# Weight sums made and split ahead, gated sums on VectorE, eight x tiles: a talking-heads attention with a two-layer feed-forward

## The chip, the core and the metric

The kernel runs on one core of one Trainium2 chip. The metric is the device time of one execution in microseconds; where several runs were timed, their median. The profile is of one execution, and its span runs from the first to the last instruction.

## What is computed

Four batches, 12 heads, 448 positions, head size 64; then 1792 tokens of width 768 and a hidden width of 2048, all in float32:

```python
scores = scale * np.matmul(q, k.transpose(0, 1, 3, 2))
scores = np.einsum('bhij,hg->bgij', scores, w_pre)
scores = scores - np.max(scores, axis=-1, keepdims=True)
attn = np.exp(scores)
attn = attn / (np.sum(attn, axis=-1, keepdims=True) + 1e-09)
attn = np.einsum('bhij,hg->bgij', attn, w_post)
x = np.matmul(attn, v)            # heads side by side: [1792, 768]
...
h = x @ w_in
g = np.where(h >= 1, h, np.where(h <= -1, 0.0, (h + 1) ** 2 / 4))
return g @ w_out
```

The two weights of the feed-forward, w_in and w_out, arrive as float64.

## The kernel before, in words

The order of the work on every engine is the order in which the code issues it: nothing is rescheduled. Each engine runs its own instructions strictly in that order, and nearly all transfers are issued by SyncE (SP in the profile), whose queue is in order too: a transfer that waits for a tile to come free holds all that are issued after it. A tile's name stands for a ring of buffers; whoever takes a new one waits until the one before it in that buffer has been read.

**Attention** runs over 16 tiles of up to 120 query positions, cut into 48 groups of mostly four blocks. A block's scores come back from the buffer `ssb` through `load_s` (a ring of eight), are mixed over heads (`pre`), get a maximum and exponentials, and are mixed again (`post`); `pv` makes x, which goes to DRAM as `xd`. Beside this, w_in and part of w_out are converted from float64 to float32 (`conv_units`, then `late_units` during the first product), and written to the DRAM arrays `wid` and `wod`.

**Split products.** TensorE multiplies float32 values as a high and a low part. A split is one ScalarE operation (high part) and one VectorE operation (low part, the value less its high part); a product is then three matmuls: low by high, high by low, high by high.

**The first product**, x @ w_in, runs in two passes (`ph`) over the halves of the tokens. A pass has 16 steps, one for each 128 of the hidden columns; a step is two halves of 448 tokens (`ffn1`), 18 matmuls each, and the gate (`gate`: one ScalarE, two VectorE operations per half), whose output goes to the tiles `gq`. Step s also splits the weights of step s+2 (`split_w`: wh on ScalarE, wl on VectorE) and loads those of step s+3 (`load_w`, tile wi). The x tiles of a pass are six for each half; `load_x` brings a raw tile xr from `xd`, through a ring of two, and `split_x` makes xh and xl. Those of pass 1 are loaded and split in step 15, when pass 0's are no longer read. Products go to eight PSUM banks in turn.

**The second product**, g @ w_out, is done as seven products of quarter matrices (`PROD`: A are quarters of the gated values, B of w_out). Each product runs through 14 items: two halves of the inner dimension, seven pairs of token blocks each. An item is 12 matmuls of 384 columns (`mults`). `prep_s` prepares an item's left side three items ahead: the split into sgh and sgl, and, for some products, a sum or difference of quarters on GpSimd (POOL), of which two overwrite a quarter of `gq` that later products read. `prep_t` prepares the right side in four quarters z per product: it loads one to four pieces of `wod`, adds them up on VectorE and splits the sum with `split_pair`, at items 1 and 4 of each half, four quarters ahead. `evict` adds a finished product into the results and stores them.

## Time and profile before

| | us |
|---|---|
| median of 3 timed runs | 989.46 (987.29 to 989.78) |
| profiled execution | 985.9 |
| its span, first to last instruction | 984.2 |
| attention, until the first product runs alone | 0 to 471.5 |
| first product, pass 0 | to about 583 |
| first product, pass 1 | to 716.1 |
| second product | 719.7 to 980.4 |
| mean granted TensorE clock (1.00 is 2.4 GHz, 0.50 is 1.2 GHz) | 0.967 |

Times in the profile count from the span's start. A matmul's shown duration is its way through the array, and matmuls overlap; their pace is read from the distance of their starts. A window counts each instruction that lies in it even partly.

### The profile page before, as it was taken

The numbers are of one execution on the slowest core, as the hardware profiler recorded it, in microseconds if no ns is written. First come the engines' busy times: TensorE is split into PE (matmuls) and PEld (weight loads), VectorE is DVE, ScalarE is ACT, GpSimd is POOL, SyncE is SP. The second block draws the span as 40 slices with busy tenths as digits, with TensorE's granted clock in tenths as the row PEclk, the third lists the DMA queues.
The fourth block names the chain that finished last, engine by engine and source line by source line (L and its number), as shares of the span: only waits on it lengthen the run. The fifth ranks groups of instructions, "written<-read, shape, count | busy, mean of one in ns | idle before, by whom it ended". The sixth has DMA issues, their size and how long they took to land.

```text
span 984.2 us, 17942 instructions
## 1 busy us (share of the span) xinstructions
PE 927.3 (94%) x6554; PEld 817.5 (83%) x6554; DVE 644.3 (65%) x1128; ACT 505.3 (51%) x1112; POOL 278.9 (28%) x309
## 2 busy tenths in 40 slices
PE   8999999999999999998999988999989877999758
PEld 7788888788887888887999976999989777998658
DVE  4878786776878777754576744444399567656344
ACT  4777777677776777665454423223245123434021
POOL 0343343433443333321122210000069686000000
PEclk9999999999999999999999996999999978999979
DMA  8758567865787657525666533121121342312442
GB/s 170 226 165 222 178 198 224 214 203 180 220 235 208 188 186 229 173 79 157 185 188 201 168 106 105 49 65 49 33 65 33 129 149 91 106 57 97 145 153 72
DMA packets 139930, 145.09 MB, mean 147 GB/s; under 512 B 63300, under 2 KB 131652, under 8 KB 139844
## 3 DMA queue, kind: packets, MB, share of 16 engines
q1 hardware_dynamic: 137060, 143.27, 48.5%
q10 hardware_dynamic: 2784, 0.69, 0.4%
q8 instruction: 52, 0.85, 0.4%
q14 instruction: 34, 0.28, 0.1%
HBM read 81.80 MB, written 23.59 MB: 107 GB/s over the span
## 4 chain that ended last, share of the span: by engine, by line
PE 79%; DMA 10%; DVE 5%; ACT 2%; issue 2%; SPq 1%; POOL 1%; DVEq 0%; ACTq 0%
PE ps_h L409 23%; PE ps_a L232 14%; PE ps_o L520 13%; PE ps_l L201 8%; PE ps_x L248 8%; PE ps_s L156 6%; DMA wo<-wod 5%; PE ps_l L199 5%; DVE wo L484 2%; DMA xr<-xd 1%; DMA s<-ssb 1%; DVE sgl L499 1%; ACT wh L376 1%; DVE wl L377 1%; PE ps_t L139 1%
## 5 line engine op out<-in xcount | busy, mean ns | idle before, releaser
L222 POOL TENSOR_SCALAR wr<-wpost,rs 120x120 f32<-120x120 f32 x180 | 113.3, 646 | 297.8 <-DVE rs L218 274.6
L520 PE MATMUL ps_o<-wh,sgl 128*128 128x384 f32 x392 | 139.5, 356 | 36.7 <-DVE sgl L499 25.6
L232 PEld LDWEIGHTS ps_a<-wr,e 120*112 120x112 f32 x1440 | 154.6, 177 | 6.9 <-issue 5.0
L232 PE MATMUL ps_a<-wr,e 120*112 120x120 f32 (+1 forms) x1440 | 155.4, 266 | 0.0
L409 PE MATMUL ps_h<-xh,wl 128*128 128x448 f32 x384 | 143.3, 373 | 5.6 <-ACT xh L395 5.6
L409 PE MATMUL ps_h<-xl,wh 128*128 128x448 f32 x384 | 143.3, 373 | 0.4 <-DVE xl L396 0.4
L409 PE MATMUL ps_h<-xh,wh 128*128 128x448 f32 x384 | 142.6, 371 | 0.0
L520 PE MATMUL ps_o<-wl,sgh 128*128 128x384 f32 x392 | 138.5, 353 | 2.4 <-DVE wl L377 2.4
L211 ACT ACTIVATE e<-ps_l,nm 120x448 f32<-120x448 f32 x180 | 112.8, 632 | 52.6 <-DVE nm L205 52.4
L520 PE MATMUL ps_o<-wh,sgh 128*128 128x384 f32 x392 | 137.6, 351 | 0.0
L520 PEld LDWEIGHTS ps_o<-wh,sgl 128*128 128x128 f32 x392 | 79.1, 202 | 40.9 <-DVE sgl L499 28.6
L205 DVE TENSOR_REDUCE nm<-ps_l 120x1 f32<-120x448 f32 x180 | 102.9, 616 | 9.3 <-PE ps_l L201 7.7
L417 ACT ACTIVATE a<-ps_h,c 128x448 f32<-128x448 f32 x64 | 40.1, 633 | 120.4 <-PE ps_h L409 73.6
L418 DVE TENSOR_TENSOR mx<-ps_h,a 128x448 f32<-128x448 f32 x64 | 39.9, 623 | 91.6 <-ACT a L417 91.0
L201 PE MATMUL ps_l<-s,wpre 120*120 120x448 f32 x196 | 95.4, 570 | 4.6 <-DMA s<-ssb 3.3
L302 POOL TENSOR_TENSOR wt<-wt,wk 128x384 int32<-128x384 int32 x64 | 70.8, 1109 | 92.3 <-DVE wt L298 54.3
L234 ACT ACTIVATE aT<-ps_a 112x480 f32<-112x480 f32 x180 | 95.6, 594 | 2.2 <-PE ps_a L232 1.8
L376 ACT ACTIVATE wh<-wo 128x768 fp32r<-128x768 f32 x28 | 23.6, 842 | 121.5 <-DVE wo L484 93.1
L409 PEld LDWEIGHTS ps_h<-xh,wl 128*128 128x128 f32 x384 | 73.6, 192 | 14.3 <-ACT xh L395 8.2
L248 PE MATMUL ps_x<-aT,v 112*64 112x120 f32 (+1 forms) x1536 | 83.8, 262 | 0.2 <-ACT aT L234 0.2
L520 PEld LDWEIGHTS ps_o<-wl,sgh 128*128 128x128 f32 x392 | 78.7, 201 | 3.9 <-DVE wl L377 3.9
L499 DVE TENSOR_TENSOR sgl<-gq,sgh 128x512 fp32r<-128x512 f32 x84 | 77.3, 953 | 4.5 <-ACT sgh L498 4.4
(83 smaller groups left out, 1576.5 us busy)
## 6 DMA issues: line engine op xcount, KB each, us to landing
s<-ssb SPq DMA_DIRECT2D x172, 210.0 KB
wo<-wod SPq DMA_DIRECT2D x56, 384.0 KB
wraw<-in_moe_w_in_dram SPq DMA_DIRECT2D x32, 384.0 KB
wi<-wid SPq DMA_DIRECT2D x32, 384.0 KB
raw<-in_moe_w_out_dram SPq DMA_DIRECT2D x20, 384.0 KB
wid<-wt SPq DMA_DIRECT2D x32, 192.0 KB
wod<-wt SPq DMA_DIRECT2D x32, 192.0 KB
v<-in_v_dram SPq DMA_DIRECT2D x12, 448.0 KB
```

The costliest lines, as they stand in the source:

```text
L156: nc.tensor.matmul(out=ps[s][:n], lhsT=qt[t][x][r, hp, :n], rhs=kt[b, hp][y][r, :], start=(m == 0), stop=(m == 2))
L201: nc.tensor.matmul(out=lps[m], lhsT=wpre[:k], rhs=x[:k], start=True, stop=True)
L205: nc.vector.tensor_reduce(out=nm, in_=lps[m], axis=AX.X, op=ALU.max, negate=True)
L211: nc.scalar.activation(out=e, in_=ps, func=AF.Exp, bias=nm, accum_out=sm[:, j:j + 1])
L222: nc.gpsimd.tensor_scalar_mul(out=w[:, :, :ni], in0=wpost[:, :, :ni], scalar1=rs[:, j:j + 1])
L232: nc.tensor.matmul(out=ps[:, r, :ni * H], lhsT=e[:, r * KP:(r + 1) * KP], rhs=w[:, :, :ni], start=True, stop=True)
L234: nc.scalar.activation(out=aT[t][:, :, :, c:c + ni], in_=ps[:, :, :ni * H].rearrange("q r (h i) -> q r h i", h=H), func=AF.Copy)
L248: nc.tensor.matmul(out=ps[s * D:(s + 1) * D, m, :n], lhsT=vt[b, g][:, 2 * m + s, r * D:(r + 1) * D], rhs=a[:, r, 4 * g + 2 * m + s, :n], s ...
L302: nc.gpsimd.tensor_tensor(out=st["t"], in0=st["t"], in1=st.pop("k"), op=ALU.add)
L409: nc.tensor.matmul(out=ps[:, :NH], lhsT=w[:, k], rhs=x, start=(c == 0), stop=(c == last))
L499: nc.vector.tensor_tensor(out=lo, in0=src, in1=hi.bitcast(F32), op=ALU.subtract)
L520: nc.tensor.matmul(out=o, lhsT=x[:, f, :], rhs=y[:, c], start=first and f == 0 and m == 0, stop=hf == 1 and f == 3 and m == 2, skip_group_ ...
```

## The change

1. *Weight sums.* In pass 1 of the first product, from step 17 to step 29, `t_units` makes the sums of quarters of w_out that four of the seven products need: eight rows of four units. A unit adds two raw tiles in place, so that each sum grows out of the one before, splits it into a tile x (ring of two), and the unit after it stores both parts to a new DRAM array `td`; the raw tile that it used up is loaded for the next row. In the second product `prep_t` only loads the two parts for these products. For the three products with a single quarter the load is issued two quarters earlier (`load_t`), and the split stays.
2. *Sums of gated values* are made on VectorE, one for each item of five of the seven products, three of them after and two before the split; which quarter is overwritten by what is rearranged so that each product needs one sum.
3. *x tiles.* For pass 1 eight raw x tiles are loaded at the end of step 12 (six in a new ring, two in the old), the last four during step 15 into the new ring. For pass 0 the first half's x tiles are loaded behind the score loads of a group, and the second half's all together into a ring of six, and split later. The conversion of w_out now ends at step 12.
4. *The join.* The first items and quarters of the second product are prepared in steps 30 and 31 ahead of the gates of those steps, and the lead is four items instead of three. The split tiles of gated values have seven buffers instead of six.

```diff
+    td = dram.tile([7, 2, NF // 4, 128, 2, CW], F32, name="td")
...
     def prep_t(k, z):
-        f = 2 * z
-        terms = PROD[k][2]
-        t = traw(terms[0][0], f, "r", 2)
-        for name, sg in terms[1:]:
-            y = traw(name, f, "ra", 2)
-            nc.vector.tensor_tensor(out=t, in0=t, in1=y, op=ALU.add if sg > 0 else ALU.subtract)
-        tset[k, z] = split_pair(t)
+        if len(PROD[k][2]) == 1:
+            tset[k, z] = split_pair(tset[k, z])
+            return
+        tset[k, z] = [pool['w'].tile([128, DM], F32R, tag="w" + c, name="w" + c, bufs=4) for c in "hl"]
+        for c, t in enumerate(tset[k, z]):
+            nc.sync.dma_start(out=t.bitcast(F32), in_=td[k, c, z].rearrange("p f d -> p (f d)"))
...
+        def store():
+            if made:
+                k, f, x = made.pop()
+                nc.sync.dma_start(out=td[k, :, f // 2, :, f % 2, :].rearrange("h p d -> p h d"), in_=x.bitcast(F32))
+
+        def make(f, k, o, u, v, sg, nxt):
+            def unit():
+                if k == 3 and f == 0:
+                    for name in ("B12", "B22", "B11", "B21"):
+                        load(name, f)
+                x = pool['tq'].tile([128, 2, CW], F32R, tag="x", name="x", bufs=2)
+                o_ = raws[o]
+                nc.vector.tensor_tensor(out=o_, in0=raws[u], in1=raws[v], op=ALU.add if sg > 0 else ALU.subtract)
+                nc.scalar.activation(out=x[:, 0], in_=o_, func=AF.Copy, scale=2.0 ** -8)
+                nc.vector.scalar_tensor_tensor(out=x[:, 1], in0=o_, scalar=2.0 ** -8, in1=x[:, 0].bitcast(F32),
+                                               op0=ALU.mult, op1=ALU.subtract)
+                store()
+                made.append((k, f, x))
+                for name in nxt:
+                    load(name, f + 1)
+            return unit
+
+        for f in range(NF // 2):
+            us.append(make(f, 3, "B12", "B22", "B12", -1, ()))
+            us.append(make(f, 2, "B11", "B12", "B11", 1, ("B12",)))
+            us.append(make(f, 4, "B22", "B22", "B11", -1, ("B22",)))
+            us.append(make(f, 6, "B21", "B11", "B21", -1, ("B11", "B21")))
+        us.append(store)
...
+        def sums(o, x, y, op):
+            nc.vector.tensor_tensor(out=o, in0=x, in1=y, op=op)
         if kind == "S2":
             src = pool['f2'].tile([128, 4, 128], F32, tag="s2", name="s2", bufs=2)
-            nc.gpsimd.tensor_tensor(out=src, in0=a22, in1=a11, op=ALU.subtract)
+            sums(src, a22, a11, ALU.subtract)
+        if kind == "S1":
+            sums(a21, a21, a22, ALU.add)
...
         if kind == "A11":
-            nc.gpsimd.tensor_tensor(out=a11, in0=a11, in1=a21, op=ALU.subtract)
+            sums(a11, a11, a21, ALU.subtract)
         if kind == "A12":
-            nc.gpsimd.tensor_tensor(out=a21, in0=a21, in1=a22, op=ALU.add)
-        if kind == "S2":
-            nc.gpsimd.tensor_tensor(out=a12, in0=a12, in1=src, op=ALU.subtract)
+            sums(a12, a12, a22, ALU.subtract)
+        if kind == "S3":
+            sums(a12, a12, a11, ALU.add)
...
-            cvs(ncv * (s + 0.5) / (NF - 1))
-            gate(s, 0, h)
+            cvs(ncv * (s + 0.5) / NV)
+            if s == te:
...
+                load_t(*tops[0])
+                load_t(*tops[1])
             if last:
                 for kk in range(KDM):
                     split_x(ph + 1, 0, kk)
-                    z = kk + 2
-                    load_x(ph + 1, z // KDM, z % KDM)
-            if s == NS - 1:
-                prep_t(0, 0)
-            gate(s, 1, h1)
+                    if kk >= 2:
+                        load_x(ph + 1, 1, kk, "xq", KDM)
+            if s >= te:
+                prep_t(*tops[s - te])
+                load_t(*tops[s - te + 2])
+                for j in ((0, 1), (2,))[s - te]:
+                    prep_s(j)
+            gate(s, 0, h)
+            if s >= ts:
+                tuns(ntu * (s - ts + 0.5) / (te - ts))
...
+            gate(s, 1, h1)
+            if s >= ts:
+                tuns(ntu * (s - ts + 1) / (te - ts))
+            cvs(ncv * (s + 1) / NV)
+            if f == NV - 1 and ph + 1 < PH:
...
+                for kk in range(KDM):
+                    load_x(ph + 1, 0, kk, "xq", KDM)
+                for kk in range(2):
+                    load_x(ph + 1, 1, kk)
```

Here NV is 13, ts 17 and te 30.

How instructions move is seen in the order on the engines. On SyncE's queue at the end of attention (s10 are score tiles, xr raw x tiles, wi a weight tile of the first product), before:

```order
L387 DMA xr_6395<-xd_75 128x448
L387 DMA xr_6397<-xd_75 128x448
L370 DMA wi_6399<-wid_76 128x768
L180 DMA s10_6401<-ssb_5936 108x1x448
L180 DMA s10_6403<-ssb_5936 120x1x448
L180 DMA s10_6405<-ssb_5936 108x1x448
L264 DMA xd_75<-xo_6158 768x1x120
```

and after the change:

```order
L374 DMA wi_6395<-wid_76 128x768
L184 DMA s10_6397<-ssb_5936 108x1x448
L184 DMA s10_6399<-ssb_5936 120x1x448
L184 DMA s10_6401<-ssb_5936 108x1x448
L391 DMA xr_6403<-xd_75 128x448
L391 DMA xr_6405<-xd_75 128x448
L268 DMA xd_75<-xo_6158 768x1x120
```

The two x loads have moved from ahead of the last three score loads to behind them.

On VectorE a step of pass 1 of the first product (wl is the low part of a weight tile, mx and gq the gate), before:

```order
L377 SCALAR_TENSOR_TENSOR wl_7962<-wi_7911,wh_7961 128x768
L418 TENSOR_TENSOR mx_7968<-ps_h_7923,a_7967 128x448
L419 SCALAR_TENSOR_TENSOR gq_6745<-a_7967,mx_7968 128x448
L418 TENSOR_TENSOR mx_7973<-ps_h_7942,a_7972 128x448
L419 SCALAR_TENSOR_TENSOR gq_6745<-a_7972,mx_7973 128x448
```

and after, with b the raw quarters and x the split sums:

```order
L381 SCALAR_TENSOR_TENSOR wl_7974<-wi_7923,wh_7973 128x768
L422 TENSOR_TENSOR mx_7980<-ps_h_7935,a_7979 128x448
L423 SCALAR_TENSOR_TENSOR gq_6749<-a_7979,mx_7980 128x448
L517 TENSOR_TENSOR b_7984<-b_7986,b_7984 128x384
L519 SCALAR_TENSOR_TENSOR x_7992<-b_7984,x_7992 128x384
L517 TENSOR_TENSOR b_7988<-b_7984,b_7988 128x384
L519 SCALAR_TENSOR_TENSOR x_7996<-b_7988,x_7996 128x384
L422 TENSOR_TENSOR mx_8004<-ps_h_7954,a_8003 128x448
L423 SCALAR_TENSOR_TENSOR gq_6749<-a_8003,mx_8004 128x448
L517 TENSOR_TENSOR b_7986<-b_7986,b_7988 128x384
L519 SCALAR_TENSOR_TENSOR x_8008<-b_7986,x_8008 128x384
```

Two or three units now stand between the gates of a step, each an addition and, behind ScalarE's high part, a low part.

On VectorE at the join of the two products (wl from wo is the low part of a weight quarter, sgl that of an item), before:

```order
L418 TENSOR_TENSOR mx_8710<-ps_h_8671,a_8709 128x448
L419 SCALAR_TENSOR_TENSOR gq_6748<-a_8709,mx_8710 128x448
L377 SCALAR_TENSOR_TENSOR wl_8717<-wo_8714,wh_8716 128x768
L418 TENSOR_TENSOR mx_8721<-ps_h_8690,a_8720 128x448
L419 SCALAR_TENSOR_TENSOR gq_6748<-a_8720,mx_8721 128x448
L377 SCALAR_TENSOR_TENSOR wl_8734<-wo_8731,wh_8733 128x768
L499 TENSOR_TENSOR sgl_8738<-gq_6741,sgh_8737 128x512
L499 TENSOR_TENSOR sgl_8743<-gq_6741,sgh_8742 128x512
```

and after, from step 31 on:

```order
L381 SCALAR_TENSOR_TENSOR wl_8970<-wo_8903,wh_8969 128x768
L555 TENSOR_TENSOR sgl_8976<-gq_6745,sgh_8975 128x512
L545 TENSOR_TENSOR gq_6745<-gq_6745 128x4x128
L422 TENSOR_TENSOR mx_8981<-ps_h_8931,a_8980 128x448
L423 SCALAR_TENSOR_TENSOR gq_6752<-a_8980,mx_8981 128x448
L422 TENSOR_TENSOR mx_8986<-ps_h_8950,a_8985 128x448
L423 SCALAR_TENSOR_TENSOR gq_6752<-a_8985,mx_8986 128x448
L555 TENSOR_TENSOR sgl_8996<-gq_6745,sgh_8995 128x512
L545 TENSOR_TENSOR gq_6745<-gq_6745,gq_6749 128x4x128
```

The second quarter and the third item stand ahead of the last two gates; the fourth item (sgl_8996) stands behind them.

## Rows read from the trace of the kernel before

**Rows 1.** The page, busy time of each engine and its share of the span

```profile
PE 927.3 (94%) x6554; PEld 817.5 (83%) x6554; DVE 644.3 (65%) x1128; ACT 505.3 (51%) x1112; POOL 278.9 (28%) x309
```

**Rows 2.** Windows, first product: PE and weight load busy (count), clock, DMA share, GB/s

```profile
471.50:582.75 111.25, 111.25 (x549) 103.11 (x550) 1.00 0.57 175
471.50:716.11 244.61, 238.63 (x1134) 216.68 (x1134) 0.97 0.37 113
```

**Rows 3.** Timeline of PE, end of the first product: start, duration

```profile
715.74 0.37 PE L409 MATMUL ps_h<-xh,wh 128*128 128x448 f32 x1
```

**Rows 4.** Chain of waits at the pass change: start, duration, what

```profile
587.64 2.54 DMA xr<-xd
...
590.21 0.58 ACT xh L395
...
590.81 0.64 DVE xl L396
```

**Rows 5.** Windows, second product, a stretch without waits; columns as rows 2

```profile
843.00:873.00 30.00, 30.00 (x175) 30.00 (x175) 1.00 0.28 90
```

**Rows 6.** Chain of waits from the last gate to the end

```profile
716.20 0.64 ACT a L417
...
789.75 1.67 POOL s L495
...
793.93 4.96 DMA wo<-wod
...
802.36 1.75 DVE sgl L499
...
888.15 1.87 DMA out_dram<-osb
...
918.29 0.97 DVE wo L484
...
919.28 3.09 DMA wo<-wod
...
923.50 0.85 ACT wh L376
...
925.34 0.60 DVE sgl L499
925.94 0.47 DVE u L552
...
980.44 0.55 DVE u L555
```

**Rows 7.** Waits of PE from 400 us: total, times, longest

```profile
PE ps_l L201 <- DMA s<-ssb: 2.6, 1, 2.6
```

**Rows 8.** Waits of SyncE's queue, 420 to 475 us; columns as rows 7

```profile
SPq L387 <- DVE xl L396: 22.3, 5, 10.1
```

**Rows 9.** Windows, end of attention: PE, PEld, DVE, ACT, POOL busy, clock, DMA share, GB/s

```profile
445.88:451.19 5.31, 2.73 (x42) 2.42 (x41) 0.97 (x3) 4.27 (x11) 0.00 (x0) 1.00 0.85 252
451.19:455.19 4.00, 4.00 (x9) 2.33 (x10) 3.41 (x8) 1.01 (x3) 2.84 (x3) 0.57 0.68 169
```

**Rows 10.** Chain of waits, the round of attention before that

```profile
442.05 0.94 PE ps_l L201 x2
...
444.36 1.51 PE ps_a L232 x15
```

**Rows 11.** Windows inside pass 0 and pass 1; columns as rows 9

```profile
500.00:560.00 60.00, 60.00 (x298) 55.60 (x297) 42.70 (x68) 29.20 (x52) 16.89 (x13) 1.00 0.58 177
620.00:700.00 80.00, 80.00 (x397) 74.15 (x396) 37.03 (x55) 22.06 (x33) 0.00 (x0) 1.00 0.18 55
```

**Rows 12.** Timeline of DVE, a step of pass 1: start, duration

```profile
622.01 0.62 DVE L418 TENSOR_TENSOR mx<-ps_h,a 128x448 f32<-128x448 f32 x1 [2.36 <-ACT a L417]
622.67 0.62 DVE L419 SCALAR_TENSOR_TENSOR gq<-a,mx 128x448 f32<-128x448 f32 x1
623.22 0.95 DVE L377 SCALAR_TENSOR_TENSOR wl<-wi,wh 128x768 fp32r<-128x768 f32 x1
```

## What the change should do to the time

> **What bounds the kernel now.** I read the page's head first: over a span of 984.2 us TensorE is busy 94% and no other engine passes 65% [rows 1]. So TensorE's gaps, and the slow clock behind them, are what an edit can win, and I measured each stage against TensorE's own full pace.
>
> First product: 549 matmuls in 111.25 us, 0.2027 us each at granted clock 1.00 [rows 2]. From 471.50 to 716.11, the end of its last matmul [rows 3], 1134 matmuls take 244.61 us [rows 2]; at 0.2027 they need 229.9. The missing 14.7 us sit at the change from pass 0 to pass 1. The chain of waits shows there six turns of the same shape: load of an x tile 2.54 us, high part on ScalarE 0.58, low part on VectorE 0.64, next load [rows 4]. With two raw x tiles, each load waits for a split.
>
> Second product: 175 matmuls in 30.00 us of a stretch without waits, and the matmuls there start 0.1733 us apart (a matmul across a window's edge is counted in it, so 173 full ones), clock 1.00 [rows 5]. Its 1176 matmuls (seven products of 14 items, 12 matmuls an item) need 203.8 us. From 716.11 to the last matmul's end at 980.44 [rows 6] pass 264.3: 60.5 us are lost. The chain names who is late: loads of weight quarters 3.09 to 4.96 us, their sums on VectorE 0.97 each, a sum of gated values on GpSimd 1.67, and a low part on VectorE of 1.75 beside it, where the same operation takes 0.60 later [rows 6].
>
> End of attention: the list of waits gives TensorE 2.6 us for the last score tiles, whose loads stand on SyncE's queue behind x loads that wait for splits, one of them 10.1 us [rows 7, 8]. When TensorE resumes, the clock is 0.57 and the seven matmuls take 4.00 us [rows 9]; the same seven took 2.31 in the round before (442.05 to 444.36) [rows 10]. Lost: 2.6 + 1.7 = 4.3 us.
>
> **The change, part by part.** *Attention's end.* The last score loads now stand ahead of the x loads that wait. All 4.3 us go. Four x tiles of the second half are now split behind the last evictions of attention instead of two; the first of the four is late by about one VectorE split, 0.64 [rows 4], of which I take 0.4. Gain 3.9.
>
> *Pass change.* Eight x tiles are loaded three steps (21.9 us) ahead, and the remaining four behind the first splits. Six splits of 0.64 take 3.9 us, and each may start when the first half of step 15 has let its tile go; the second half of that step runs 3.65 us (18 x 0.2027) beside them, and VectorE's splits for the first half of step 16 end before TensorE wants them, those for its second half about 2 us before. Gain 14.7; were the loads not there, all of it would stay. The conversion of w_out, now in 13 steps instead of 15, adds 15% to its part of VectorE's work; VectorE is busy 42.70 of 60.00 us in that pass [rows 11], so there is room.
>
> *Weight sums.* Out of the second product go 28 additions and the splits of 16 quarters, and quarters that come split need only loads. Into pass 1 go 32 units in 13 steps, 2.46 a step. A unit is an addition on 384 columns, about half of 0.97; a high part on ScalarE, about 0.58 x 384/448 = 0.50; a low part on VectorE, half of 0.95 [rows 4, 6, 12]. VectorE waits inside the unit, so the unit costs it 0.49 + 0.50 + 0.48 and two handovers of 0.03, 1.53 us. A step there has already wl 0.95 and two gates of 0.66 + 0.55 (from start to start) [rows 12], 3.37. Sum: 3.37 + 2.46 x 1.53 = 7.13, and three places where VectorE waits for a ScalarE operation queued behind the unit's (gate 0.64 against 0.48, twice; wh 0.85 against 0.48 [rows 6]): 0.69. That makes 7.8 us a step, while TensorE needs 36 x 0.2027 = 7.30. So VectorE falls behind by 0.5 a step, 7 over 13 steps; with about 1 that it brings along from the pass change, L = 8 us. TensorE doesn't notice during the pass: the weight split is made two steps ahead, 14.6 us less its own 0.95, and the gates have eight banks.
>
> It notices at the join. The first quarter of the second product is loaded on SyncE behind the last stores of weight sums, and those wait for VectorE. With T the end of the first product, the last unit ends at T - 14.6 + L. Then store and load issue 0.8, landing 3.1, ScalarE 0.85, VectorE 0.95: T - 8.9 + L. Behind that on VectorE: two splits with sums 2.4, two gates 2.4, wl 0.95, a split with its sum 1.2, two gates 2.4, and the split of the fourth item 0.6: T + 1.05 + L. TensorE wants the fourth item at T + 3 x 2.08 = T + 6.2. The stall is L - 5.1, about 3 us, and the slow clock behind it another 1.7, by the stretch at the end of attention [rows 9, 10]. At L of 5 or less it is nothing; at 13.6, where the split starts to hold TensorE in the pass, 8.5 + 1.7. I take 4.8.
>
> *DMA.* A unit loads 192 KB and stores 384. With 2.46 units and one wi a step that is 253 GB/s (2.46 x 590 + 393 kB in 7.30 us). Around 446 us the trace has 252 GB/s at a DMA share of 0.85, and in pass 1 now 55 GB/s at 0.18 [rows 9, 11]. So it fits, narrowly. A raw quarter is wanted about two unit intervals less one unit after its load is due: 2 x 7.30/2.46 - 1.53 = 4.4 us, against two issues and 2.5 us of landing (2.54 for an x tile of similar size), 3.3. The store that frees x's buffer has the same 4.4 against 3.0 (1.87 for half the bytes [rows 6], 0.4 of issue, 0.7 for the other half). Cover 1.1 and 1.4 us.
>
> By the Trainium skill, DMA: Bandwidth & Descriptors, section Latency and other measured facts, HBM's access latency is 0.2 us on average and 2 us at high load. The trace agrees in direction: 3.09 us quiet against 4.96 among other transfers [rows 6]. By that rule the cover goes, and the time is that of the second rival.
>
> *Sums of gated values on VectorE.* Now 0.60 each, as a split without GpSimd beside it [rows 6], one per item. In the products S1 and S2 the sum stands ahead of the high part: 0.60 + 0.67 (ScalarE, 0.58 x 512/448) + 0.60 and handovers, 1.93 us against 12 x 0.1733 = 2.08 of TensorE. In their second halves the addition into the result, 0.47, joins, and in S1's two wl: 2.4 and 2.67. The excess of at most 0.6 x 7 = 4.2 us is hidden by four items prepared ahead, 8.3 us; without that cover it is the price. *Loads of split quarters* have three items, 6.2 us, against 0.5 for the eviction ahead on SyncE, 0.8 for two issues and 3.1 to 4.96 to land: up to 0.1 late each, I take 0.5 for all.
>
> **The sum.** Profiled execution 985.9 us (span 984.2 and 1.7 around it). 985.9 - 3.9 - 14.7 - 60.5 + 4.8 + 0.5 = 912.1. The median of the timed runs lies 3.6 above the profiled execution (989.46); with that, 916 us.
>
> **The rivals.** *VectorE keeps up* (L of 5 or less): instructions that don't wait overlap a little on both engines (gq to wl starts after 0.55 where gq takes 0.62 [rows 12]). Then 4.8 falls away: 911 us. Against it stands the addition above.
>
> *DMA takes the place of the wait.* If transfers in pass 1 land as the slow one does, 1.9 us later, each of 16 loads that a next row's sums want is 0.8 late and each of 32 stores 0.5: 29 us on VectorE's queue, L = 37. TensorE is held 37 - 13.6 = 23 us in the pass, and 10 at the join: 911 + 33 = 944 us; half that lateness gives about 926. For it: 253 GB/s is as much as this trace ever moves. Against: wi's loads and the conversions of pass 0 run at 177 GB/s and a share of 0.58 with no TensorE wait [rows 11].
>
> *The pass change stays*, because the eight loads are late: 916 + 14.7 = 931 us. Against: 21.9 us of lead for eight loads of 2.5 even one by one.
>
> *Slower than before:* every unit waits for its store and the next row's load in turn, since x has two buffers and each raw quarter one: 1.53 + 3.0 + 3.3 = 7.8 us a unit, 250 us for 32 where the 13 steps last 95. After 13.6 us of cover the rest, 141, holds TensorE, and 10 more at the join: 1062 us. It decides from about 5.6 us a unit, (95 + 13.6 + 79 - 10)/32. Against: the queue holds several transfers at once, and no unit depends on the store of the one just before it.
>
> **Chances.** Forecast (912 to 921) 0.50; VectorE keeps up 0.25; DMA 0.18; pass change stays 0.04; slower 0.03. The range 906 to 936 takes in the first two, half of the third and the fourth. Within 0.3%, about 3 us, a measurement of this kernel can't tell a change; no case but a chance mixture ends there: faster 0.96, same 0.01, slower 0.03.
>
> **What would show it.** Right: no x load in the chain around the pass change; VectorE busy over 80% between steps 17 and 29 with its gates ever later behind TensorE's banks; one TensorE wait of some 3 us within the first four items of the second product, with a lower clock behind it; no GpSimd work and no further wait of over 1 us after that; low parts at 0.60 throughout. Wrong: TensorE waits for wl inside pass 1 (DMA rival; the additions then wait for loads); waits in S1 or S2 on a low part; a second product well over 210 us.

## The result and the profile after

The changed kernel takes **922.11 us** (median of 4 runs, 920.56 to 922.84), the kernel before on the same chip 989.56: a ratio of 0.9321, 95% interval 0.9303 to 0.9339. The prediction said 916, within 906 to 936: the sign and the range hold, the forecast's own case (912 to 921) ends 1 us below the median. The two errors that this hides are told further down: the sum for the profiled execution was 912.1, and the profiled execution took 922.84.

Busy times on the page of the changed kernel, to be read beside [rows 1]:

```profile
PE 904.9 (98%) x6554; PEld 800.4 (87%) x6554; DVE 646.3 (70%) x1218; ACT 510.0 (55%) x1128; POOL 181.0 (20%) x253
```

TensorE has the same 6554 matmuls and is busy 98% of a span of 921.1 us. VectorE has 90 instructions more and the same busy time. The windows of the changed kernel (columns as [rows 9]):

```profile
466.93:702.87 235.94, 235.05 (x1134) 212.45 (x1134) 164.76 (x271) 99.67 (x180) 24.41 (x20) 1.00 0.61 195
590.00:697.00 107.00, 106.31 (x515) 96.26 (x514) 78.28 (x132) 40.07 (x72) 0.00 (x0) 1.00 0.67 218
630.00:650.00 20.00, 20.00 (x98) 18.18 (x97) 15.21 (x27) 7.25 (x13) 0.00 (x0) 1.00 0.77 252
702.87:917.22 214.35, 209.08 (x1176) 208.25 (x1176) 141.59 (x222) 77.17 (x128) 0.00 (x0) 0.98 0.31 103
702.87:712.00 9.13, 3.88 (x12) 3.38 (x13) 8.54 (x13) 6.75 (x13) 0.00 (x0) 0.63 0.22 52
...
600.00:680.00 80.00, 80.00 (x389) 72.64 (x388) 57.55 (x99) 29.93 (x53) 0.00 (x0) 1.00 0.71 231
```

The first product alone, 244.61 us before [rows 2], takes 235.94 (first row). From its end to the last matmul's end, 264.3 before, pass 214.35 (fourth row). The transfers of the weight sums lift pass 1 from 55 GB/s [rows 11] to 218 (second row), in one stretch of 20 us to 252 (third row). What is left of TensorE's waits, from 400 us on, and then what ScalarE and VectorE wait for from 580 to 702 us (columns as [rows 7]):

```profile
PE ps_o L576 <- DVE wl L381: 3.3, 1, 3.3
PE ps_o L576 <- DVE sgl L555: 1.9, 1, 1.9
PE ps_h L413 <- DVE wl L381: 0.7, 1, 0.7
PE ps_a L236 <- POOL wr L226: 0.6, 1, 0.6
PE ps_h L413 <- DVE xl L400: 0.2, 1, 0.2
...
ACT x L518 <- DMA td<-x: 12.8, 6, 3.0
...
DVE x L519 <- ACT x L518: 26.0, 32, 1.8
```

The wait for score tiles [rows 7] and the chain of x loads at the pass change [rows 4] are gone; two waits at the join are new, and nothing in the second product waits after them. The row of ScalarE is the one that the forecast does not have: six times the high part of a weight sum waits for the store `td<-x` that must leave its buffer. The chain of waits of the changed kernel, first in pass 1 and then at the join (start, duration, what):

```profile
651.95 4.86 DMA td<-x
...
656.97 0.54 ACT x L518
...
657.53 0.56 DVE x L519
...
685.46 4.52 DMA td<-x
...
697.55 0.57 DVE x L519
698.12 0.02 issue
698.14 0.36 SPq L508
698.55 3.73 DMA wo<-wod
...
702.30 0.85 ACT wh L380
...
704.06 0.69 DVE sgl L555
...
709.30 0.96 DVE wl L381
710.26 0.04 issue
710.31 19.76 PE ps_o L576 x98
```

The reader is to see the whole price of the lateness here: a store of 4.52 us holds up a unit; the last unit ends at 698.12; the store and the load of the first weight quarter follow on SyncE; its parts are there at 704.1, 1.3 us after the first product's end at 702.87; and the second quarter's low part ends at 710.26. TensorE's timeline shows which matmuls wait (start, duration):

```profile
704.80 0.44 PE L576 MATMUL ps_o<-wh,sgl 128*128 128x384 f32 x1 [1.93 <-DVE sgl L555]
...
706.47 0.52 PE L576 MATMUL ps_o<-wh,sgl 128*128 128x384 f32 x1
710.31 0.69 PE L576 MATMUL ps_o<-wl,sgh 128*128 128x384 f32 x1 [3.32 <-DVE wl L381]
```

Between the two waits are seven matmuls. It is the eighth matmul of the *first* item that stands 3.32 us for the second quarter, not the fourth item.

### The profile page after: what moved, and what is told of

Its sections match the earlier page's. It is cut to its first block, busy times and chain, and to the rows that moved or that the text cites. A ratio compares the mean times of both kernels' runs of the same rounds, so it can differ in the third digit from the quotient of the medians.

```text
span 921.1 us, 18118 instructions
## 1 busy us (share of the span) xinstructions
PE 904.9 (98%) x6554; PEld 800.4 (87%) x6554; DVE 646.3 (70%) x1218; ACT 510.0 (55%) x1128; POOL 181.0 (20%) x253
## 4 chain that ended last, share of the span: by engine, by line
PE 76%; DMA 8%; DVE 7%; issue 3%; ACT 3%; SPq 1%; POOL 0%; ACTq 0%; DVEq 0%; POOLq 0%
PE ps_o L576 22%; PE ps_a L236 14%; PE ps_h L413 13%; PE ps_x L252 8%; PE ps_l L205 7%; PE ps_s L160 6%; PE ps_l L203 5%; DMA td<-x 3%; DMA s<-ssb 2%; ACT x L518 1%; DVE x L519 1%; DVE wl L381 1%; DVE mx L422 1%; PE ps_t L143 1%; DVE b L517 1%
## 5 line engine op out<-in xcount | busy, mean ns | idle before, releaser
L576 PE MATMUL ps_o<-wl,sgh 128*128 128x384 f32 x392 | 133.1, 340 | 3.3 <-DVE wl L381 3.3
L576 PE MATMUL ps_o<-wh,sgl 128*128 128x384 f32 x392 | 133.1, 340 | 1.9 <-DVE sgl L555 1.9
L576 PE MATMUL ps_o<-wh,sgh 128*128 128x384 f32 x392 | 132.9, 339 | 0.0
L554 ACT ACTIVATE sgh<-gq 128x512 fp32r<-128x512 f32 x84 | 52.1, 631 | 89.8 <-PE ps_o L576 63.8
L306 POOL TENSOR_TENSOR wt<-wt,wk 128x384 int32<-128x384 int32 x64 | 68.8, 1077 | 88.1 <-DVE wt L302 68.2
L555 DVE TENSOR_TENSOR sgl<-gq,sgh 128x512 fp32r<-128x512 f32 x84 | 57.6, 688 | 33.1 <-ACT sgh L554 33.1
L252 PEld LDWEIGHTS ps_x<-aT,v 112*64 112x64 f32 x1536 | 73.8, 137 | 6.4 <-issue 1.8
L413 PEld LDWEIGHTS ps_h<-xl,wh 128*128 128x128 f32 x384 | 72.1, 188 | 8.0 <-DVE xl L400 0.9
L413 PEld LDWEIGHTS ps_h<-xh,wh 128*128 128x128 f32 x384 | 72.1, 188 | 7.1
L576 PEld LDWEIGHTS ps_o<-wl,sgh 128*128 128x128 f32 x392 | 74.5, 190 | 3.8 <-DVE wl L381 3.8
```

Of the source, the lines that this page charges most:

```text
L252: nc.tensor.matmul(out=ps[s * D:(s + 1) * D, m, :n], lhsT=vt[b, g][:, 2 * m + s, r * D:(r + 1) * D], rhs=a[:, r, 4 * g + 2 * m + s, :n], s ...
L306: nc.gpsimd.tensor_tensor(out=st["t"], in0=st["t"], in1=st.pop("k"), op=ALU.add)
L413: nc.tensor.matmul(out=ps[:, :NH], lhsT=w[:, k], rhs=x, start=(c == 0), stop=(c == last))
L555: nc.vector.tensor_tensor(out=lo, in0=src, in1=hi.bitcast(F32), op=ALU.subtract)
L576: nc.tensor.matmul(out=o, lhsT=x[:, f, :], rhs=y[:, c], start=first and f == 0 and m == 0, stop=hf == 1 and f == 3 and m == 2, skip_group_ ...
```

## Experiments

Every variant does the whole computation. Ratios are to the kernel before on the same chip; that of the changed kernel is 0.9321. The stages in the table come from the starts of matmuls in each variant's profile: the first product alone (first to last start), from its last start to the last start of the second product, and the pace of a matmul, in us, in each. "Both" means that 0.2027 and 0.2067 occur; 0.1748 is a mean over items of two paces, as told at the end; "–" is a product without a long stretch free of waits.

| | median us | ratio, 95% interval | first product | join to end | pace 1 | pace 2 |
|---|---|---|---|---|---|---|
| before | 989.56 | 1 | 244.31 | 264.32 | 0.2027 | 0.1733 |
| before, again | 988.37 (one run) | | 244.89 | 265.82 | 0.2027 | 0.1733 |
| changed | 922.11 | 0.9321 [0.9303, 0.9339] | 235.64 | 214.35 | 0.2067 | 0.1748 |
| changed, again | 920.95 | 0.9352 [0.9331, 0.9373] | 235.50 | 214.03 | both | 0.1748 |
| three x buffers | 915.48 | 0.9304 [0.9282, 0.9325] | 234.38 | 206.85 | 0.2067 | 0.1748 |
| early loads | 913.53 | 0.9280 [0.9263, 0.9296] | 232.89 | 208.02 | 0.2027 | 0.1748 |
| earlier x splits | 919.36 | 0.9346 [0.9330, 0.9361] | 234.22 | 213.91 | both | 0.1748 |
| these three together | 909.15 | 0.9224 [0.9206, 0.9243] | 231.59 | 205.55 | 0.2027 | 0.1748 |
| no weight sums | 982.82 | 0.9970 [0.9949, 0.9990] | 231.24 | 278.71 | 0.2027 | – |
| sums on GpSimd | 920.19 | 0.9334 [0.9312, 0.9355] | 234.69 | 213.84 | both | 0.1748 |
| ring of two x tiles | 929.25 | 0.9438 [0.9406, 0.9470] | 243.64 | 214.17 | 0.2027 | 0.1748 |
| three together, one pool | 913.39 | 0.9247 [0.9219, 0.9276] | 233.97 | 208.25 | both | 0.1733 |

**The change once more.** 

> The changed kernel once more, nothing edited. In its first profile the matmuls of the first product start 0.2067 us apart from 468 to 695 us (0.2027 in the kernel before) and those of the second product 0.1748 apart (0.1733 before), at granted clock 1.00 in both. If that pace belongs to the kernel, this profile shows 0.2067 and 0.1748 again, in the same stretches, and the time is 922 us within 2. If it is a matter of one execution, at least one of the two paces comes out at the value of before, and the time of that execution is lower by 4.6 us (first product) or 1.7 us (second).

 The second profile has the same two waits at the join (1.8 and 3.8 us, where the first has 1.9 and 3.3) and the same 214 us from there on. It also shows another pace of the same program. Windows of it, columns as [rows 9]:

```profile
480.00:560.00 80.00, 80.00 (x389) 72.67 (x388) 52.67 (x84) 34.48 (x64) 21.23 (x18) 1.00 0.59 179
600.00:680.00 80.00, 80.00 (x397) 74.14 (x396) 58.06 (x99) 30.70 (x55) 0.00 (x0) 1.00 0.73 234
```

389 matmuls in pass 0, 397 in pass 1, in equal stretches without a wait at granted clock 1.00: 0.2067 us against 0.2027. In the first profile both stretches have 389. The faster pace did not shorten the first product, which takes 235.50 us here and 235.64 there: the wait for a weight's low part near its end grew from 0.7 us to 2.3.

```profile
PE ps_h L413 <- DVE wl L381: 2.3, 1, 2.3
```

TensorE got to that weight sooner, and VectorE was hardly earlier with it.

**Three x buffers.** The ring of split weight sums gets three buffers, and two raw quarters lie in an idle ring:

```diff
-                raws[name] = pool['tq'].tile([128, CW], F32, tag=name, name="b", bufs=1)
+                if name in ("B11", "B21"):
+                    raws[name] = pool['x0'].tile([128, NH], F32, tag="xr", name="b", bufs=2)[:, :CW]
+                else:
+                    raws[name] = pool['tq'].tile([128, CW], F32, tag=name, name="b", bufs=1)
...
-                x = pool['tq'].tile([128, 2, CW], F32R, tag="x", name="x", bufs=2)
+                x = pool['tq'].tile([128, 2, CW], F32R, tag="x", name="x", bufs=3)
```

> Three buffers instead of two for the split weight sums (two raw quarters move into the idle ring of x tiles, to make room). In the changed kernel ScalarE waits six times, 12.8 us in all, for a store of weight sums to land before it can write the next one. Theory A: these waits make most of VectorE's lateness; without them the last unit ends about 6 to 9 us earlier than 698, the two waits of TensorE at the join (1.9 and 3.3 us) shrink below 1 us together, and the time falls by 5 to 8 us to about 915. Rival B: VectorE is late because a unit costs it 1.7 us and more with ScalarE's part, and only the place of the waiting moves (to raw quarters that arrive late, since stores and loads share one queue); then the last unit ends at most 3 us earlier and the time falls by 0 to 3 us.

 ScalarE waits for no store any more, and the join costs TensorE a single wait:

```profile
PE ps_o L579 <- DVE wl L381: 1.1, 1, 1.1
```

The stretch from the first product's end falls from 214.03 to 206.85 us. VectorE's timeline separates the two causes of its lateness. From wl to wl over eleven steps the changed kernel takes 694.29 - 602.90 = 91.39 us, 8.31 a step; with three buffers 85.87, 7.81 a step. TensorE's step in both is 36 x 0.2067 = 7.44. These are the rows of the first and last wl of the eleven steps, first in the changed kernel and then with three buffers (start, duration):

```profile
602.90 0.96 DVE L381 SCALAR_TENSOR_TENSOR wl<-wi,wh 128x768 fp32r<-128x768 f32 x1 [0.18 <-ACT wh L380]
...
694.29 0.96 DVE L381 SCALAR_TENSOR_TENSOR wl<-wi,wh 128x768 fp32r<-128x768 f32 x1 [0.18 <-ACT wh L380]
...
600.94 0.96 DVE L381 SCALAR_TENSOR_TENSOR wl<-wi,wh 128x768 fp32r<-128x768 f32 x1 [0.18 <-ACT wh L380]
...
686.81 0.96 DVE L381 SCALAR_TENSOR_TENSOR wl<-wi,wh 128x768 fp32r<-128x768 f32 x1 [0.18 <-ACT wh L380]
```

So the units cost VectorE 0.4 us a step more than TensorE gives, and the stores another 0.5. The other profiles agree: 7.80 and 7.82 us a step in the two further ones with three buffers, 8.18 to 8.32 in the five further ones with two.

The profiled execution is the variant's best. It took 912.91 us at a mean granted clock of 1.000; the other four took 915.13 to 919.43, at 0.994 to 0.996, as the changed kernel has it. The single wait of 1.1 us is therefore not shown for the usual execution; by medians the third buffer is worth 5.5 us, which is within theory A.

**Early loads at the join.** The first two quarters of the second product are loaded ahead of the last weight sums instead of behind them:

```diff
+            if s == te - 1:
+                load_t(*tops[0])
+                load_t(*tops[1])
...
-                load_t(*tops[0])
-                load_t(*tops[1])
```

> The first two weight quarters of the second product are loaded at the beginning of step 29, ahead of the last units of weight sums on SyncE's queue, instead of behind their stores. Theory A: TensorE's two waits at the join (1.9 us for the first item's low part, 3.3 us for the second quarter's low part) and the slow clock behind them (about 3 us) come from this load, which stands behind the last stores; with the load early, VectorE's chain at the join is about 4 to 5 us shorter, the waits shrink to 0 to 1 us, and the time falls by 5 to 8 us. Rival B: VectorE's lateness alone suffices for the waits (the last unit ends 10 us after TensorE has finished step 29); then the waits shrink by 2 us at most, the clock still falls, and the time falls by 0 to 3 us.

 The wait of the first item is gone, that for the second quarter falls to 2.3 us, from 3.3 and 3.8 in the two profiles of the change; from the join on it is 6.0 us less than in the repeated change. Another 2.6 lie in the first product, where this profile has the faster pace throughout; the edit does not touch that pace, so I don't count this part as its gain. By medians it is 7.4 us faster, theory A's 5 to 8, but the wait that is left is longer than A's 1 us: VectorE's lateness alone still makes one.

**Earlier x splits.** Two of the four late splits move back ahead of the last evictions of attention:

```diff
-            put(NG + (kk > 1), lambda kk=kk: split_x(0, 1, kk))
+            put(NG + (kk > 3), lambda kk=kk: split_x(0, 1, kk))
```

> At the end of attention four x tiles of the second half are split ahead of the last evictions, as in the kernel before, instead of two. That takes away TensorE's short wait of 0.28 us at 468.4 us, right behind which the pace of the first product's matmuls goes from 0.2027 to 0.2067 us. Theory A: the pace is set by how the stream of matmuls starts after a wait, and stays until the next one; without this wait pass 0 runs at 0.2027 from the start to the pass change, which gives 0.3 + 558 x 0.0040 = 2.5 us, or up to 4.8 us if the later short wait at 586.7 does not set it. Rival B: the pace comes from where the tiles lie in memory, which this edit hardly moves; then it stays 0.2067 and the time falls by 0.3 us or not at all.

 The intervals overlap with the repeated change's; no difference is shown. The short wait at 468 us alone does not fix the slower pace: four other variants that have it (early loads, no weight sums, sums on GpSimd, ring of two) run at 0.2027 behind it. Of the three profiles without it (this one, the three together, and these with one pool) none starts at 0.2067. Pass 0 ran at 0.2027 here, as theory A said, but the time did not follow, for TensorE then waited 2.2 us in pass 1 for the low parts of weights.

**The three together.** 

> The three edits together: three buffers for the split sums, the first two quarters loaded at step 29, four x tiles split early. Theory A (VectorE's backlog at the end of the first product and the load behind the last stores make the two waits at the join): both waits go, also the 0.7 to 2.3 us for a weight split inside pass 1, and the clock does not fall behind the join. Against the changed kernel on the same chip that is 8.5 us at the join and 1 to 2 in the pass: 8 to 12 us, 909 to 913 us where the changed kernel takes 921. Rival B: each of the edits only reached the same few us, and one of them has them all; then it is no faster than the faster single one, 913.5 us, within 1.

 At 909.15 us this beats both kernels, as theory A said, and its five executions lie within 908.75 to 909.85. TensorE's waits from 440 us to the end:

```profile
PE ps_h L413 <- DVE xl L400: 1.3, 2, 0.8
PE ps_a L236 <- POOL wr L226: 0.6, 1, 0.6
```

There is no wait at the join, and 205.55 us behind it are 1176 x 0.1748: nothing is lost.

**Without the weight sums.** Loads, additions and splits stand in the second product again, as before; the gated sums stay on VectorE, the x tiles and the lead of four stay. The earlier loads of single quarters go too, and there are six split gated tiles instead of seven, to make room for the raw quarters:

```diff
-        if len(PROD[k][2]) == 1:
-            tset[k, z] = split_pair(tset[k, z])
-            return
...
+        terms = PROD[k][2]
+        t = traw(terms[0][0], 2 * z, "r", 2)
+        for name, sg in terms[1:]:
+            y = traw(name, 2 * z, "ra", 2)
+            nc.vector.tensor_tensor(out=t, in0=t, in1=y, op=ALU.add if sg > 0 else ALU.subtract)
+        tset[k, z] = split_pair(t)
...
-        tun = t_units()
+        tun = []
```

> The changed kernel without part 1: no sums in the first product, and the second product loads, adds and splits its weight quarters itself as before, at the same two items of each half (the ring of split gated values has six buffers instead of seven, for room). Theory A: in the kernel before, the stretch from 840 to 980 us, where GpSimd no longer works, needs 640 x 0.1733 = 111 us and takes 140; these 29 us are waits for weight quarters and come back here, and a little more in the two products with single quarters; the join's 8.5 us go, since VectorE is not late. Net 20 to 32 us over the changed kernel: 941 to 953 us. Rival B: the lead of four items and the sums off GpSimd would have hidden the quarters without part 1; then it stays within 5 us of the changed kernel or is faster by the join.

 It is 62.6 us slower than the variant with the sums on GpSimd on the same chip, far more than either theory gave. The first product keeps its whole gain (231.24); the second takes 278.71, longer than before. The waits of TensorE from 440 us and of VectorE in the second product:

```profile
PE ps_o L578 <- ACT wh L380: 29.8, 8, 8.7
PE ps_o L578 <- DVE sgl L557: 17.9, 7, 4.6
...
DVE wo L494 <- DMA wo<-wod: 38.8, 12, 5.7
```

VectorE stands 38.8 us in additions that wait for loads. That is hardly more than in the kernel before, from 716 us on:

```profile
DVE wo L484 <- DMA wo<-wod: 35.6, 11, 6.0
```

So the waiting itself is not new. Behind such an addition now stand the low parts and the gated sums of all coming items, where before the gated sums were on GpSimd. That the sums' place makes the extra 14 us is argued from this order, not tried by itself; the sixth buffer and the lead were not tried alone either. Without part 1 of the change (the weight sums and the earlier loads) nothing of the second product's gain is left.

**Gated sums on GpSimd.** One sum for each item as in the change, on the other engine:

```diff
-            nc.vector.tensor_tensor(out=o, in0=x, in1=y, op=op)
+            nc.gpsimd.tensor_tensor(out=o, in0=x, in1=y, op=op)
```

> The changed kernel with the sums of gated values back on GpSimd, still one for each item of five products (so the engine alone is undone, not the rearranged sums). Theory A: a sum takes GpSimd 1.67 to 1.80 us and the low part on VectorE grows from 0.69 to up to 1.75 while it runs; where one waits for the other an item costs 2.3 to 2.5 us instead of TensorE's 2.08, so 70 items lose 0.2 to 0.4 each: 12 to 28 us slower. Rival B: both engines stay below 2.08 us an item and the lead hides the rest; within 4 us of the changed kernel.

 No difference in time, though the operations are slower. Groups by line from 705 to 910 us, GpSimd's sums and VectorE's low parts (count, busy us, mean ns, idle before):

```profile
L545 POOL TENSOR_TENSOR gq<-gq 128x512 f32<-128x512 f32 x55 | 91.0, 1686 | 9.0 <-DVE sgl L555 9.0
...
L555 DVE TENSOR_TENSOR sgl<-gq,sgh 128x512 fp32r<-128x512 f32 x82 | 85.2, 1060 | 25.6 <-ACT sgh L554 25.6
```

In the changed kernel the same groups read

```profile
L555 DVE TENSOR_TENSOR sgl<-gq,sgh 128x512 fp32r<-128x512 f32 x83 | 56.9, 688 | 33.1 <-ACT sgh L554 33.1
L545 DVE TENSOR_TENSOR gq<-gq 128x512 f32<-128x512 f32 x56 | 38.6, 688 | 1.0
```

This is rival B. A low part of 1.06 us on average in place of 0.69 still fits into an item's 2.08 us; that it does because no addition waits for a load ahead of it is the likely reason, not a tried one.

**Ring of two x tiles.** The x loads of pass 1 go through two buffers again, as before:

```diff
-                    if kk >= 2:
-                        load_x(ph + 1, 1, kk, "xq", KDM)
+                    z = kk + 2
+                    load_x(ph + 1, z // KDM, z % KDM)
...
+                    if kk + 2 < KDM:
+                        load_x(ph + 1, 1, kk + 2)
...
-                for kk in range(KDM):
-                    load_x(ph + 1, 0, kk, "xq", KDM)
...
-                    load_x(ph + 1, 1, kk)
+                    load_x(ph + 1, 0, kk)
```

> The changed kernel with the x tiles of pass 1 loaded as before, through the ring of two during step 15. Theory A: the whole stall of the pass change comes back, 19.5 us in which 18 matmuls should take 3.7 and a slow clock behind it; I sized it at 14.7 us: 12 to 17 us slower. Rival B: the stall gives VectorE time to catch up, and the join's 8.5 us shrink by half or more; then 6 to 11 us slower.

 The chain at the pass change is back (a load of 2.5 us, high part, low part, next load), and TensorE's waits have a row for it again:

```profile
PE ps_h L413 <- ACT xh L399: 4.8, 4, 2.0
```

By medians the price is 9.1 us against the GpSimd variant of the same chip. By profiles of equal pace it is 10.8: 243.64 us of first product against 232.89 with early loads, each with a wait of some 1.5 us for a weight's low part. (Against the 231.24 without weight sums, where that wait is missing, it would be 12.4.) The join is no better for it (214.17 us): the stall gives VectorE no time that would help there. So rival B's reason does not hold, though the time lies in its range; theory A's chain is back, at less than its 12 us.

**The kernel before once more.** 

> The kernel before, profiled once more. Theory A: the pace of a matmul is the execution's, drawn anew at a wait of TensorE; then this profile may show another pace than the first one did: 0.2067 us in part of the first product's 1176 matmuls, or 0.1748 in the second product instead of 0.1733, and its span lies up to 6 us above 984.2. Theory B: the pace is the program's; then the first product after the join of the attention shows 0.2027 us, the second 0.1733, and the span is within 1.5 us of 984.2.

 Both paces came back, 0.2027 and 0.1733, in a span 2.4 us longer, which is more than theory B allowed and is not the pace's: 1.5 of it lie behind the join. Its 988.37 us lie within the 985.47 to 989.85 of the kernel's other executions on that chip. That the second product has 0.1748 in all profiles of the change, and 0.1733 in both of the kernel before, then speaks for the program.

**One pool for the split gated tiles.** The three together, but all six of these tiles in one pool, which is free only after the first product, so no item is prepared early:

```diff
-        p, n = (pool['sq'], NSA) if j % (NSA + NSB) < NSA else (pool['f2'], NSB)
+        p, n = pool['f2'], 6
...
-                for j in ((0, 1), (2,))[s - te]:
-                    prep_s(j)
...
-        for j in range(3, LEAD):
+        for j in range(LEAD):
             prep_s(j)
```

> All three changes together, but with the six split gated tiles of the second product in one pool, as the kernel before has them, and so the first three items prepared only after the first product. Theory A: 0.1748 us for a matmul of the second product comes from where these tiles lie, and goes back to 0.1733, 1.7 us over 1176 matmuls; against that stands a stall of TensorE at the join of some 6 to 12 us (three preparations that nothing covers, and the lower clock behind them), so 914 to 920 us. Theory B: the place of the tiles has no part in it: 0.1748 stays, and the time is 916 to 922 us.

 The pace is 0.1733 again, in every item, as theory A said. The join costs less than it said: one wait of 2.7 us, and 208.25 us from the join on, 4.4 over 1176 x 0.1733. The early items are thus worth about 4.4 us at most, and cost 1.7 by their place. Its time is not told apart from the 909.15 by intervals (0.9247 and 0.9224, which overlap), though its profile is 5.0 us longer in the span, 2.4 of them in the first product.

## Why the prediction was right, and where it was off

The sum is compared with the profiled execution, as it was made: 912.1 forecast, 922.84 measured. The 3.6 us that I added for the median went the wrong way: after's profiled execution is the slowest of its four runs, 0.7 above their median. The sum is thus 10.7 off, the 916 only 6.1; that the median's place made up 4.6 of it is luck.

| term | forecast | measured | from |
|---|---|---|---|
| attention's end | -3.9 | -4.6 | first product alone from 466.93, before from 471.50 |
| pass change and pass 1 | -14.7 | -8.7 | 235.94 against 244.61 |
| second product without join | -60.5 | -58.8 | 1176 x 0.1748 = 205.56 against 264.32 |
| join | +4.8 | +8.8 | 214.35 - 205.6 |
| loads of split quarters | +0.5 | 0 | no wait after 710.31 |

- **Attention's end**: right. The score wait is gone. The late low part of x costs 0.2 where I took 0.4: at 468.44 and 468.75 two matmuls start 0.26 and 0.31 us behind the one before, against 0.20 each. No run undoes this part alone.
- **Pass change**: the mechanism was right. With the pace of before the first product takes 231.24 us without the weight sums, 13.1 less than before, and putting the two-tile ring back costs 10.8, against the 14.7 forecast for the whole. The term missed by 6.0. The slower pace, 0.0040 us more for nearly each of 1134 matmuls, makes about 4.5 of it, a wait of 0.7 at 695.3 for a weight's low part and one of 0.2 at 586.69 for a low part of x nearly all the rest. The forecast had the latter 2 us in time; ScalarE waits 2.9 us for the x loads of step 15 just there. But pace and weight wait are not separate prices: in the repeated profile the faster pace only made the weight wait longer, and with it throughout (early loads) the first product is 2.6 to 2.8 us shorter, not 4.5.
- **The cover inside the pass** was sized too large. TensorE was to feel VectorE's lateness in pass 1 from 13.6 us on; it feels it from 10. In all six profiles with two buffers for the split sums the last unit ends 9.7 to 9.9 us late (in the prediction's measure, by which it is on time 14.6 us before the first product's end), whatever the pace, and TensorE waits 0.7 to 2.3 us in the pass for low parts of weights. So this is not how late VectorE would get if left alone, but as late as it gets before TensorE waits with it. Such a wait was among the prediction's signs of being wrong, together with additions that wait for loads; the second part did not come.
- **VectorE's step of 7.8 us**: right to the rounding where stores don't disturb, 7.81 with three buffers, 7.80 with the three edits together. What would show it was stated wrongly: VectorE is busy 73% of the window and not over 80%, because the handovers to ScalarE, 26.0 us in 32 units, show as idle.
- **The step that failed first is "cover 1.4 us" for the store that frees x's buffer.** The store was to take 3.0 us. On the chain it takes 3.68 to 5.81, and ScalarE waits 12.8 us for six of them. Lateness at the end is 10 us (last unit at 698.1, where 14.6 before the join at 702.87 would be on time) instead of L = 8, and stands at the limit just told. This is the rival in which DMA takes the place of the wait, in a small form: its stores, not its raw loads, on which VectorE never waits. The Trainium skill, DMA: Bandwidth & Descriptors, section Latency and other measured facts, gives 2 us at high load in place of 0.2 for HBM's latency; the trace agrees that the cover goes at 252 GB/s and a share of 0.77, and shows 0.7 to 2.8 more than the 3.0 forecast. What makes these stores longer, HBM or the other transfers on the queues, was not tried apart. The forecast also took 253 GB/s for the most that the trace of before ever moves; that is a misreading, for beside its slow load of a weight quarter it moves 309 (columns as [rows 9]):

```profile
793.93:798.89 4.96, 4.96 (x30) 4.96 (x30) 2.17 (x2) 0.63 (x1) 4.80 (x4) 1.00 0.97 309
```

- **The second step that failed is "TensorE wants the fourth item".** An item reads two weight quarters; the second one's low part stands on VectorE behind two splits, two sums and two gates, ready at T - 3.15 + L by the forecast's own terms, and it is wanted seven matmuls into the first item, at about T + 1. With L = 8 that is a stall of 3.8, with L = 10 5.8; measured are 1.93 + 3.32 = 5.25. The stall came twice with few matmuls between, and the clock was 0.63 on the mean from 702.87 to 712.00: the other 3.5 us of the 8.8, where I took 1.7. With a third buffer, L is about 5 and the wait 1.1 in its best execution; with the quarters loaded early too it is nothing.
- **Second product**: right. No GpSimd work, no wait, no late load of a split quarter. The low part with no GpSimd beside it takes 0.69 us, as the groups have it, where I took 0.60 (the distance to the next start in the chain; the duration in the trace of before is 0.69 too). The cover was wide enough for either. But moving the gated sums to VectorE earned nothing: on GpSimd the time is the same.

The rival that everything got slower and the one that the x loads stay late had no part. "VectorE keeps up" did not happen: VectorE falls behind even with a third buffer, by 0.4 us a step, and that variant's median is 915.48 us against the rival's 911. What comes to its time is the three edits together, 909.15.

## What to carry to other kernels

When work is moved ahead into another stage, look at the last thing that is freed by a transfer, and at the first tile wanted on the other side: here a ring one buffer too short for a store under load and two loads queued behind the last unit cost 9 of the 13 us that the combined version gets back. Ask for each operand of the first item, not for each item, when it is wanted. A wait that is removed may take others with it: with the weight sums made ahead, slow GpSimd sums, one for each item, no longer cost anything.

## What the runs showed of the chip that was not expected

**The pace of matmuls at full clock has two values, and a wait can change it.** At granted clock 1.00, matmuls of 448 columns start 0.2027 or 0.2067 us apart, for hundreds of them; the same program shows both in different executions and different stretches of one. Where it changed in the first product, there was a wait of TensorE: at 586.6 in the repeated change, at 675.07 and 692.23 with the earlier splits, about 585 with one pool. Over 1134 matmuls the difference is up to 4.5 us, so a profile of one run can't tell an edit's effect below that unless the paces are read first. What decides between the two is open.

**In the second product the pace follows the tile.** With three of seven split gated tiles in a pool of their own, three items of seven run at 0.1767 and four at 0.1733, round after round. The three edits together, starts of the first matmul of items 7, 8, 9, 10 and 11 (12 matmuls apart):

```profile
712.50 0.34 PE L579 MATMUL ps_o<-wh,sgl 128*128 128x384 f32 x1
...
714.62 0.34 PE L579 MATMUL ps_o<-wh,sgl 128*128 128x384 f32 x1
...
716.74 0.34 PE L579 MATMUL ps_o<-wh,sgl 128*128 128x384 f32 x1
...
718.86 0.33 PE L579 MATMUL ps_o<-wh,sgl 128*128 128x384 f32 x1
...
720.94 0.33 PE L579 MATMUL ps_o<-wh,sgl 128*128 128x384 f32 x1
```

The distances are 2.12 three times and then 2.08. With all of them in one pool every item takes 2.08. The variant without weight sums tells the pool from the number of buffers: it has three of six in the pool of their own, and there three items of six take 2.12, in rounds of six. The place is not all of it: in the variants with early loads or three buffers, whose first item waits, the second and third items use the same three tiles and take 2.08; only from the eighth item on they take 2.12. How place and the last wait act together was not settled.

**VectorE and GpSimd slow each other on the same kind of operands.** A low part takes 0.69 us alone, and 1.06 on average with GpSimd's sums beside it, which take 1.69 on average on GpSimd and 0.69 on VectorE. GpSimd loses as well: a sum that starts when VectorE's low part has ended takes 1.29 (start, duration):

```profile
758.18 1.29 POOL L545 TENSOR_TENSOR gq<-gq 128x512 f32<-128x512 f32 x1 [0.63 <-DVE sgl L555]
```

The Trainium skill, SBUF — State Buffer, section Who interferes with whom, says that a VectorE instruction with two inputs from SBUF contends with a GpSimd instruction that reads SBUF; the trace agrees by these figures, and the equal times show that it costs nothing where both are covered.
